# Gated linear attention with an MLP behind it: weights loaded in six parts, the quarter turn as a 128-row matmul, another order table

## The chip, the cores and the metric

The kernel runs on one core of one Trainium2 chip. The metric is the device time of one execution in microseconds, as the median of several runs; the profile is of one more execution of the same program. The engines of the core are PE (TensorE, matmuls; PEld is its loading of weights), DVE (VectorE), ACT (ScalarE), POOL (GpSimd) and SP (SyncE, which here only issues DMAs). Each engine works through its own instructions in order, and waits where an instruction needs what another engine or a DMA has yet to deliver.

## The reference

Inputs are q, k, v, a_re and a_im, each 4 x 8 x 768 x 48 (batch, heads, steps, head dimension) in fp32, a scale vector of 384 and two weight matrices of 384 x 1536 and 1536 x 384.

```python
def _attn_ref(q, k, v, a_re, a_im):
    mag = np.sqrt(a_re * a_re + a_im * a_im)
    scale = np.minimum(mag, 0.999) / (mag + 1e-06)
    a_re_n, a_im_n = (a_re * scale, a_im * scale)
    for t in range(S):
        new_re = ar * S_re - ai * S_im          # ar, ai: step t of a_re_n, a_im_n
        new_im = ar * S_im + ai * S_re
        S_re, S_im = (new_re + k_t v_t^T, new_im)
        y[:, :, t] = q_t @ S_re
...
def _moe_ref(x, g_ln, w_ch1, w_ch2):
    xn = (x - mu) / np.sqrt(var + 1e-06) * g_ln
    return x + np.maximum(xn @ w_ch1, 0.0) @ w_ch2
```

So a complex decay, one number for each head dimension and step, multiplies a state of 48 x 48 for each head; the real part of the state is read by q. The 8 heads side by side make rows of 384, which go through a layer norm, a two-layer MLP with ReLU, and a residual sum.

## The kernel before

**Tiling.** The 768 steps of a batch are cut into 6 chunks of 128 steps. Two chunks make a pair, so there are 3 pairs in a batch and 12 pairs (P = 0 to 11) in all, 24 chunks (n = 0 to 23). Each pair goes through the same stages; pair 0 is split in two halves of 4 heads for the elementwise ones (`PARTS`), so its names have .0 and .1.

**Stages of a pair**, by the names in the code:
- Loads by SP: `are`, `aim` (384 KB each for a pair), `q`, `k`, `vf` (192 KB for each chunk).
- Decay, magnitude: `ln` and `iv` on ACT (log of a_re, and its inverse by Exp), `r` (a_im / a_re), `r2`, `u` (Ln of 1 + r2, ACT), `l` and `lc` (log of the magnitude, capped, DVE), `dec` (PE, sums over the steps with triangular ones `u_e`), `en` and `e` (ACT, Exp with either sign).
- Decay, angle: `th` (Arctan, ACT), `ph` (PE, sums with `u_th`, in turns, on top of what `pick` takes from `car`, the carry of the pair before), `car` (the carry for the next pair), `sin` (ACT, Sin of the fraction of a turn read as int16), and for `cos` in pairs 0 to 3 (`QUARTER`) `qt`: a matmul that adds a quarter turn to `ph` in place, after which ACT takes Sin again. Pairs 4 to 11 use `abs` and a bias instead.
- `ke`, `qe` (k and q times the decay), `ks`, `qs` (times cos and sin, stacked as 48 + 48 rows of 128), each on DVE or POOL.
- Each chunk: `kT`, `qT` (transposes on PE) and `ksT`, `qsT` (their copies out of PSUM by DVE or ACT), or instead `ksT`, `qsT` as one transposing DMA issued by SP; `am` (8 matmuls), `atm` (times the causal mask, DVE), `gm` and `G` (state), `y` (attention output in PSUM), `x` (copy of it), `bn` (statistics), `xtr` and `xT` (transposed x).
- MLP of a pair: `mm1` in three groups of two blocks (6 matmuls of 128 x 256 each), `relu` for each group on ACT or DVE, `mm2` for each chunk in three blocks of 4 matmuls of 128 x 384, `oa` and `ot` (scale by `rstd` and add x), `st` (store).
- `dps`, `decc` take the whole decay of a pair to the state.

**Weights.** `w1b` and `w2b` hold both matrices in bf16; `wl.0` and `wl.1` load them (and cast) by one DMA each, issued by POOL. `wp` (PE) multiplies w1 by the scale vector's mean matrix `gc`, `wc` (DVE, nine instructions at L388) scales w1 and subtracts the result; mm1 of group j needs the three `wc.j`.

**Order.** Nothing is scheduled at run time. A table (`PLAN`) lists every operation by name with its engine (P, A, V, G, S for PE, ACT, DVE, POOL, SP) and, after the letter, its PSUM bank; `Graph.run` emits them in that order, so the table is the order of each engine's queue. `@name` makes an operation wait for another on top of its data (some POOL operations take turns with DVE so). `tab.log` and `tab.trig` are loads of ACT's function table: Ln and Exp need the one, Arctan and Sin the other. `warm` are fillers: a matmul of 128 x 256 on constants whose result nobody reads; they need `u_e` alone. Buffers are rings (`RINGS`, 2 to 10 of a kind).

The start of the table before, in short: pair 1's `are` first, its ln and iv, pair 0's ln and iv, a trig load with Arctan and Sin of half of pair 0, a log load, a trig load, and so on: four log and four trig loads up to pair 2's second Sin. `wl.0` is issued after `v.0`, `wl.1` after `ks.1.0.0`; all of `wp` and `wc` follow pair 0's `y`.

Of the kernel before, what the change touches and what calls it, by code (L numbers as in the profile page):

```python
# [54 lines left out]
warm.67:P4 warm.68:P4 warm.69:P4 qt.0.0:P3 dps.0:P2 cos.0.0:A3 cos.0.1:A0 ks.0.0.1:V ks.0.0.0:V ks.0.1.0:V
qs.0.1.0:V ph.1.0:P4 dec.1.0:P6 qs.0.0.0:V warm.70:P1 warm.71:P1 qT.1:P3 tab.log.2:A en.1.0:A6 u.2.0:A
ln.3.0:A iv.3.0:A e.1.0:A6 v.0:G@qs.0.0.0 decc.0:V2 ks.0.1.1:V vf.1.1:S vf.1.0:S q.2.0:S car.1.0:V4
warm.72:P1 warm.73:P1 kT.0:P2 qT.0:P1 kT.1:P0 qsT.1:V3 tab.trig.2:A sin.1.0:A4 ksT.0:V2 wl.0:G ksT.1:V0
am.1:P2 gm.0:P0 ke.1.0.1:G@ks.0.1.1 ke.1.0.0:G th.2.0:A qsT.0:V1 am.0:P6 dps.1:P1 decc.1:A1 qt.1.0:P4
l.2.0:V r.3.0:V lc.2.0:V G.0:V0 gm.1:P0 cos.1.0:A4 dec.2.0:P4 k.2.1:S tab.log.3:A e.2.0:A4 en.2.0:A4  # L60
atm.0:V6 atm.1:V2 G.1:V0 r2.3.0:V k.2.0:S are.4.0:S ph.2.0:P6 y.1:P1 aim.4.0:S ks.1.0.1:G@lc.2.0 x.1:V1
are.5.0:S ks.1.0.0:G y.0:P2 kT.3:P3 x.0:V2 ksT.3:V3 u.3.0:A tab.trig.3:A sin.2.0:A6 wp.2:P0 wc.2.1:V0
wc.2.0:V0 xtr.0:P1 wl.1:G xtr.1:P4 wp.0:P5 wp.1:P2 wc.2.2:V0 xT.1:V4 qt.2.0:P6 xT.0:A1 kT.2:P3 th.3.0:A
cos.2.0:A6 wc.0.2:V5 wc.0.1:V5 wc.1.2:V2 wc.0.0:V5 wc.1.1:V2 ksT.2:A3 mm1.0.2.1:P0 mm1.0.2.0:P0
qe.1.0.0:G@r2.3.0 qe.1.0.1:G qs.1.0.0:G relu.0.2:A0 ph.3.0:P6 qs.1.0.1:G qe.2.0.1:G qT.2:P3 qT.3:P4
car.3.0:A6 mm1.0.0.1:P0 mm1.0.0.0:P0 wc.1.0:V2 qsT.3:V4 sin.3.0:A6 qt.3.0:P6 qsT.2:A3 mm1.0.1.0:P4 l.3.0:V
lc.3.0:V qe.2.0.0:V aim.5.0:S v.1:G pad.qs.2:G am.3:P2 mm1.0.1.1:P4 cos.3.0:A6 bn.0:V bn.1:V relu.0.0:A0
qs.2.0.0:G@qe.2.0.0 k.3.0:S q.3.1:S relu.0.1:A4 gm.2:P6 rstd.0:G am.2:P0 mm2.0.0:P7 dec.3.0:P4 G.2:A6
atm.3:V2 y.3:P2 tab.log.4:A e.3.0:A4 x.3:A2 vf.2.0:S vf.2.1:S k.3.1:S gm.3:P6 atm.2:V0 qs.2.0.1:V y.2:P3
mm2.0.1:P7 qT.4:P2 xtr.3:P0 mm2.1.0:P1 mm2.0.2:P7 en.3.0:A4 mm2.1.1:P1 qT.5:P4 ln.4.0:A iv.4.0:A xT.3:A0  # L70
ln.5.0:A x.2:V3 dps.3:P3 ke.2.0.0:V ke.2.0.1:G ks.2.0.1:V ks.2.0.0:G@ks.2.0.1 kT.4:P5 xtr.2:P0 are.6.0:S
r.4.0:G q.3.0:S vf.3.0:S mm2.1.2:P1 bn.2:V bn.3:V iv.5.0:A rstd.1:A r.5.0:G r2.4.0:A decc.3:A3 ot.0:V7
G.3:V6 qsT.4:V2 xT.2:V0 mm1.1.2.1:P6 ksT.4:V5 qsT.5:V4 kT.5:P0 ot.1:V1 mm1.1.2.0:P6 qe.3.0.1:G ke.3.0.0:G
v.2:G mm1.1.0.1:P4 mm1.1.0.0:P4 ksT.5:V0 am.4:P2 am.5:P0 ke.3.0.1:G u.4.0:A relu.1.2:V6 mm1.1.1.1:P6
mm1.1.1.0:P6 relu.1.0:V4 mm2.2.0:P4 r2.5.0:A u.5.0:A tab.trig.4:A th.4.0:A relu.1.1:A6 th.5.0:A atm.5:V0
ph.4.0:P0 atm.4:V2 k.4.0:S y.4:P5 mm2.2.1:P4 ks.3.0.0:G ks.3.0.1:V l.4.0:V lc.4.0:V mm2.3.0:P6 mm2.3.1:P6
gm.4:P7 mm2.3.2:P6 abs.4.0:A0 sin.4.0:A0 qe.3.0.0:V qs.3.0.0:V qs.3.0.1:V dec.4.0:P2 vf.3.1:S st.0:S G.4:V7
x.4:V5 tab.log.5:A ln.6.0:A oa.3:A6 q.4.0:S v.3:G@qs.3.0.1 car.4.0:A0 mm2.2.2:P4 qT.6:P5 xtr.4:P7 y.5:P6
k.4.1:S q.4.1:S e.4.0:A2 l.5.0:V en.4.0:A2 qsT.6:V5 ot.3:G@l.5.0 ph.5.0:P0 aim.6.0:S x.5:V6 lc.5.0:V
xtr.5:P5 gm.6:P6 dps.4:P2 ot.2:V4 kT.6:P3 xT.5:V5 xT.4:A7 iv.6.0:A qe.4.0.0:G are.7.0:S ke.4.0.0:G@lc.5.0  # L80
ke.4.0.1:G r.6.0:G tab.trig.5:A cos.4.0:A ks.4.0.0:G qe.4.0.1:G decc.4:V2 mm1.2.0.1:P4 ks.4.0.1:G abs.5.0:A0
mm1.2.0.0:P4 qsT.7:S sin.5.0:A0 r2.6.0:A th.6.0:A ksT.6:V3 qs.4.0.0:G G.6:V6 mm1.2.1.0:P2 mm1.2.1.1:P2
gm.7:P6 ksT.7:S bn.5:V st.2:S relu.2.0:V4 G.7:V6 relu.2.1:V2 cos.5.0:A tab.log.6:A ln.7.0:A mm1.2.2.1:P0
mm1.2.2.0:P0 mm2.4.0:P7 mm2.5.0:P6 am.6:P4 bn.4:V rstd.2:A am.7:P2 mm2.4.1:P7 relu.2.2:V0 mm2.4.2:P7
dec.5.0:P0 atm.7:V2 iv.7.0:A u.6.0:A atm.6:V4 kT.8:P2 y.7:P3 k.5.0:S y.6:P4 e.5.0:A0 vf.4.0:S vf.4.1:S
are.8.0:S v.4:G q.5.0:S q.6.0:S st.1:S aim.7.0:S k.5.1:S x.6:A4 qe.5.0.0:G@l.6.0 mm2.5.1:P6 mm2.5.2:P6
ksT.9:S x.7:A3 q.5.1:S vf.5.0:S st.3:S aim.8.0:S en.5.0:A0 ksT.8:A2 qs.4.0.1:V l.6.0:V lc.6.0:V xtr.7:P5
qT.8:P4 xtr.6:P3 xT.6:V3 gm.8:P0 qT.9:P1 xT.7:A5 G.8:A0 oa.5:A6 dec.6.0:P2 r.7.0:G@lc.6.0 qsT.8:V4 am.8:P4
ln.8.0:A e.6.0:A2 ot.4:V7 en.6.0:A2 bn.7:V atm.8:V4 gm.9:P0 mm1.3.2.0:P6 G.9:V0 qsT.9:V1 mm1.3.2.1:P6
mm1.3.1.1:P4 y.8:P2 mm1.3.1.0:P4 k.6.1:S am.9:P0 dps.6:P3 bn.6:V iv.8.0:A relu.3.2:A6 ke.5.0.0:G vf.5.1:S  # L90
k.6.0:S q.6.1:S x.8:V2 st.4:S are.9.0:S xtr.8:P2 mm1.3.0.1:P6 mm1.3.0.0:P6 atm.9:V0 r2.7.0:A ke.5.0.1:G
u.7.0:A relu.3.1:A4 ks.5.0.1:V decc.6:V3 qe.5.0.1:V r.8.0:V relu.3.0:A6 ph.6.0:P0 vf.6.0:S y.9:P3 mm2.6.0:P4
mm2.7.0:P5 mm2.7.1:P5 x.9:A3 xtr.9:P3 mm2.6.1:P4 mm2.6.2:P4 l.7.0:V lc.7.0:V ks.5.0.0:V qs.5.0.0:V
tab.trig.6:A sin.6.0:A0 qs.5.0.1:V rstd.3:G xT.8:A2 ot.5:G th.7.0:A qT.10:P2 xT.9:V3 ke.6.0.0:V car.6.0:V0
abs.6.0:V0 mm2.7.2:P5 ph.7.0:P6 mm1.4.2.0:P0 qe.6.0.1:G@ke.6.0.0 qsT.10:A2 mm1.4.0.0:P2 mm1.4.0.1:P2
mm1.4.2.1:P0 sin.7.0:A6 bn.8:V r2.8.0:A cos.6.0:A qe.6.0.0:G qs.6.0.1:G v.5:G abs.7.0:V6 car.7.0:V6
relu.4.0:A2 mm1.4.1.0:P6 mm1.4.1.1:P6 th.8.0:A ot.6:V4 relu.4.2:V0 ot.7:V5 dec.7.0:P2 ksT.10:S gm.10:P4
am.10:P0 tab.log.7:A e.7.0:A2 relu.4.1:V6 mm2.8.0:P5 mm2.8.1:P5 ke.6.0.1:G qs.6.0.0:G ks.6.0.1:G ksT.11:S
qsT.11:S st.5:S mm2.8.2:P5 am.11:P6 bn.9:V ks.6.0.0:V G.10:A4 ln.9.0:A vf.6.1:S k.7.1:S aim.9.0:S en.7.0:A2
v.6:G@ks.6.0.0 mm2.9.0:P4 rstd.4:G atm.10:V0 dps.7:P2 y.10:P3 gm.12:P0 iv.9.0:A atm.11:V6 r.9.0:V mm2.9.1:P4  # L100
u.8.0:A x.10:A3 l.8.0:V G.12:A0 xtr.10:P1 y.11:P3 mm2.9.2:P4 q.8.0:S gm.13:P0 decc.7:A2 st.6:S q.7.0:S
bn.10:V r2.9.0:G@l.8.0 xT.10:A1 x.11:A3 lc.8.0:V G.13:V0 k.7.0:S q.7.1:S xtr.11:P6 oa.9:A4 vf.7.0:S xT.11:A6
ph.8.0:P2 qT.12:P4 qsT.12:V4 abs.8.0:V2 mm1.5.2.0:P6 mm1.5.0.1:P0 mm1.5.0.0:P0 tab.trig.7:A cos.7.0:A
sin.8.0:A2 qT.13:P4 mm1.5.2.1:P6 mm1.5.1.0:P2 relu.5.0:A0 mm2.10.0:P0 mm1.5.1.1:P2 bn.11:V ksT.13:S
# [702 lines left out]
```

## Time and profile before

| | |
|---|---|
| median of 3 runs | 193.94 us (193.87 to 194.18) |
| span of the profiled execution | 191.7 us, 5125 instructions |
| granted TensorE clock over the span | 0.986 |
| PE busy | 175.3 us (91%), 2039 matmuls |
| ACT busy | 165.2 us (86%), 234 instructions |
| DVE busy | 154.8 us (81%), 267 instructions |
| POOL busy | 109.2 us (57%), 124 instructions |
| table loads on ACT (L775) | 23, 29.5 us |
| fillers on PE (L770) | 74, 10.5 us |
| DMA by SP's queue | 34.88 MB, 87.7% of 16 engines' span |
| DMA by POOL's queue (weights) | 2.36 MB, 7.3% |

How to read it: spans are from the first to the last instruction of that execution. Busy times are unions, so an engine's instructions may overlap and add up to more. A matmul's duration contains its latency; in a row of matmuls the distance from start to start is shorter. Time an engine stands idle costs only where something late follows from it. In the groups, a line with "out<-in (shape) xN | busy, mean" gives the mean duration in ns of one instruction, and what ended the idle time ahead of them. In the windows, each engine has its busy time within a stretch and, after it, the number of its instructions; PEclk is the granted clock as a share of the full one.

### The profile page before, as it was taken

The page shows a single profiled execution, that of the slowest core. Times are in us where ns is not written, and L with a number is a line of the kernel's source. Part 1 is how long each engine was busy: PE and PEld are TensorE (multiplying, and loading weights), DVE is VectorE, ACT ScalarE, POOL GpSimd, SP SyncE. Part 2 cuts the span into 40 slices and gives each one's busy share as a digit, 9 for nine tenths or more (in the row PEclk, how much of TensorE's full clock was granted, in tenths as well). Part 3 has the DMA queues.
Part 4 walks back from the last instruction along what each step waited for, and adds up shares of the span by engine and source line. Part 5 has one row for each costly group of instructions (what it writes and reads, how often), then busy time and mean ns, then how long its engine had stood idle before and what let it go on. Part 6 is the DMA issues. An engine that isn't in the chain of part 4 may idle for free.

```text
span 191.7 us, 5125 instructions
## 1 busy us (share of the span) xinstructions
PE 175.3 (91%) x2039; PEld 132.7 (69%) x2039; DVE 154.8 (81%) x267; ACT 165.2 (86%) x234; POOL 109.2 (57%) x124
## 2 busy tenths in 40 slices
...
GB/s 151 291 244 219 236 190 203 168 218 298 184 212 237 166 163 255 192 258 211 161 169 265 167 255 152 184 288 253 204 228 153 208 145 144 248 103 165 3 129 118
DMA packets 132104, 37.56 MB, mean 196 GB/s; under 512 B 127088, under 2 KB 131696, under 8 KB 132080
## 3 DMA queue, kind: packets, MB, share of 16 engines
q1 hardware_dynamic: 130128, 34.88, 87.7%
q0 software_dynamic: 1952, 2.36, 7.3%
q8 instruction: 16, 0.26, 0.5%
...
## 4 chain that ended last, share of the span: by engine, by line
PE 38%; ACT 27%; DVE 16%; issue 8%; DMA 4%; POOL 3%; SPq 1%; DVEq 0%; POOLq 0%; ACTq 0%
PE banks L741 14%; PE banks L720 9%; ACT h L731 5%; ACT L775 4%; DVE w1b L388 3%; DMA qsT<-qs 3%; PE banks L477 2%; PE banks L616 2%; DVE l L466 2%; ACT r L462 2%; ACT en L481 2%; PE banks L496 2%; PE banks L593 2%; ACT r L458 2%; DMA are<-in_a_re_dram 2%
## 5 line engine op out<-in xcount | busy, mean ns | idle before, releaser
L741 PE MATMUL banks<-w2b,h 128*128 128x384 bf16 x288 | 54.9, 326 | 0.3 <-ACT h L731 0.2
L720 PE MATMUL banks<-xT,w1b 128*128 128x256 bf16 x432 | 51.9, 272 | 0.8 <-ACT trig L514 0.5
L720 PEld LDWEIGHTS <-w1b 128*128 128x128 bf16 x432 | 41.2, 98 | 7.7 <-DVE xT L291 1.3
L741 PEld LDWEIGHTS <-h 128*128 128x128 bf16 x288 | 26.0, 97 | 14.3 <-ACT h L731 0.8
L294 DVE TENSOR_TENSOR atm<-banks,mask 128x1024 bf16<-128x1024 f32 x24 | 28.7, 1217 | 5.2 <-PE banks L616 2.8
L731 ACT ACTIVATE h<-banks 128x1024 bf16<-128x1024 f32 x24 | 24.1, 1023 | 8.7 <-PE banks L720 8.5
L775 ACT ACT_TABLE_LOAD x23 | 29.5, 1283 | 1.2 <-PEq L791 0.8
L294 POOL TENSOR_TENSOR ks<-ke,trig 128x768 bf16<-128x768 bf16 x14 | 22.8, 1640 | 8.8 <-DVE ke L294 2.8
L294 POOL TENSOR_TENSOR qs<-qe,trig 128x768 bf16<-128x768 bf16 x11 | 18.0, 1641 | 12.3 <-DVE ot L755 5.0
L294 POOL TENSOR_TENSOR ke<-k,en 128x384 bf16<-128x384 f32 x18 | 16.5, 930 | 11.8 <-DMA vf<-in_v_dram 10.3
L294 POOL TENSOR_TENSOR qe<-q,e 128x384 bf16<-128x384 f32 x16 | 14.6, 921 | 12.2 <-ACT e L481 5.9
L733 DVE TENSOR_SCALAR h<-banks 128x1024 bf16<-128x1024 f32 x12 | 14.5, 1215 | 4.9 <-PE banks L720 4.9
L753 POOL TENSOR_TENSOR ot<-ot,x 128x384 f32<-128x384 f32 x8 | 7.3, 916 | 14.6 <-ACT ot L746 13.6
L616 PE MATMUL banks<-qsT,ksT 128*128 128x128 bf16 x192 | 14.3, 219 | 1.4 <-DVE ksT L291 1.2
L616 PEld LDWEIGHTS <-ksT 128*128 128x128 bf16 x192 | 12.1, 98 | 3.4 <-DVE ksT L291 1.4
L496 PE MATMUL banks<-th,u_th 128*128 128x384 f16 (+1 forms) x52 | 12.4, 325 | 2.2 <-ACT th L485 2.2
L679 DVE BATCH_NORM_STATS2 stats<-x 128x6 f32<-128x384 bf16 x24 | 13.1, 547 | 0.0
L755 DVE SCALAR_TENSOR_TENSOR ot<-banks,rstd,x 128x384 f32<-128x384 f32 x16 | 9.6, 609 | 4.1 <-DMA out_dram<-ot 2.9
L466 DVE SCALAR_TENSOR_TENSOR l<-r,w 128x768 f16<-128x768 f16 (+1 forms) x13 | 11.5, 892 | 1.6 <-ACT r L462 1.6
L770 PE MATMUL banks<-u_e 128*128 128x256 f16 x74 | 10.5, 302 | 2.2 <-POOL u_e L328 2.2
L477 PE MATMUL banks<-l,u_e 128*128 128x384 f16 (+1 forms) x52 | 10.4, 327 | 2.2 <-DVE l L469 1.3
L448 ACT ACTIVATE w<-are 128x768 f32<-128x768 f32 (+1 forms) x13 | 10.3, 796 | 2.2 <-DMA are<-in_a_re_dram 2.2
...
## 6 DMA issues: line engine op xcount, KB each, us to landing
...
```

The lines of the kernel that those rows point to most:

```text
L294: {"DVE": nc.vector, "POOL": nc.gpsimd}[eng(name)].tensor_tensor(**kw)
L466: nc.vector.scalar_tensor_tensor(out=S_("l"), in0=S_("r2"), scalar=0.5, in1=S_("w"), op0=ALU.mult, op1=ALU.add)
L477: nc.tensor.matmul(heads(ps[:, c]), lhsT=u_e[:, c, j], rhs=step(T("l", P), j), start=(j == 0), stop=(j == R - 1))
L496: nc.tensor.matmul(heads(ps[:, c]), lhsT=u_th[:, c, j], rhs=step(T("th", P), j), start=False, stop=(j == R - 1), skip_group_check=True)
L616: nc.tensor.matmul(ps[:, h], lhsT=T("ksT", n)[:, h], rhs=T("qsT", n)[:, h], start=True, stop=True)
L679: nc.vector.bn_stats(out=T("stats", n), in_=T("x", n))
L720: nc.tensor.matmul(ps[:, jj], lhsT=w1b[:, dc, ts(gi * JG + jj, C)], rhs=T("xT", P)[:, dc].rearrange("p c t -> p (c t)"), start=(dc == 0), ...
L731: act(out=dst, in_=src, func=AF.Relu)
L733: nc.vector.tensor_scalar(out=dst, in0=src, scalar1=0.0, scalar2=None, op0=ALU.max)
L741: nc.tensor.matmul(bank(f"o.{n}")[:, 0:DM], lhsT=T("h", P)[:, j, ts(c, C)], rhs=w2b[:, j], start=(j == 0), stop=(j == NJ - 1))
L770: g.add(f"warm.{i}", lambda i=i: nc.tensor.matmul(bank(f"warm.{i}")[:, 0:256], lhsT=u_e[:, 0, 0], rhs=u_e[:, 1].rearrange("p j t -> p (j t ...
L775: g.add(f"tab.{nm}.{i}", lambda tab=tab: nc.scalar.preload_act_table_set(tab))
```

## The change

Five things are changed, the last of them in the table alone:

1. `wl` becomes six DMAs: `wl.0` to `wl.2` load a third of w1's columns each, `wl.3` to `wl.5` a third of w2's rows. `wp.j` needs only `wl.j`, and block `part` of mm2 only `wl.(3 + part)`.
2. `qt` uses all 128 rows of `pick` and `qrow` instead of row 64 alone; `qrow` is therefore set to zero first.
3. 72 fillers are defined, and the table holds all 72; it held 74.
4. Table loads have one running number in the order table; there are 19 of them.
5. The order table is another one: order, engines and banks. Transposes by DMA are 22 (25 before), stacks transposed on PE 26 (23); `ksT` on DVE 11 (6), on ACT 1 (4); `decc` all 8 on DVE (5 of 8 on ACT before); `relu` 26 on ACT, 10 on DVE (24, 12); `car` 6 on ACT, 3 on DVE (3, 6); `v` 4 on DVE, 1 on ACT, 7 on POOL (1, 3, 8); smaller shifts in others.

The old names wl.0 and wl.1 stood for whole matrices; the new ones are parts.

```diff
-    g.add("qrow", lambda: nc.gpsimd.memset(qrow[ds(HALF, 1)], 0.25), needs=["ue"])
+    g.add("qrow", lambda: [nc.gpsimd.memset(qrow, 0.0), nc.gpsimd.memset(qrow[ds(HALF, 1)], 0.25)],
+          needs=["ue"])
...
-    g.add("wl.0", lambda: nc.gpsimd.dma_start(
-        out=w1b, in_=moe_w_ch1.rearrange("(dc p) j -> p dc j", p=C)))
-    g.add("wl.1", lambda: nc.gpsimd.dma_start(
-        out=w2b, in_=moe_w_ch2.rearrange("(jc p) e -> p jc e", p=C)))
+    for i in range(NG):
+        g.add(f"wl.{i}", lambda i=i: nc.gpsimd.dma_start(
+            out=w1b[:, :, ts(i, 512)], in_=moe_w_ch1.rearrange("(dc p) j -> p dc j", p=C)[:, :, ts(i, 512)]))
+        g.add(f"wl.{NG + i}", lambda i=i: nc.gpsimd.dma_start(
+            out=w2b[:, ts(i, JG)], in_=moe_w_ch2.rearrange("(jc p) e -> p jc e", p=C)[:, ts(i, JG)]))
...
-        g.add(o, wp, needs=["wgc", "wl.0"], ps=(o, 1))
+        g.add(o, wp, needs=["wgc", f"wl.{jb}"], ps=(o, 1))
...
-                        nc.tensor.matmul(ps[:, c], lhsT=pick[ds(HALF, 1)], rhs=qrow[ds(HALF, 1), 0:W],
+                        nc.tensor.matmul(ps[:, c], lhsT=pick, rhs=qrow[:, 0:W],
...
-                    needs=[f"relu.{P}.{part}", "wl.1"] + ([f"mm2.{n}.{part - 1}"] if part else []),
+                    needs=[f"relu.{P}.{part}", f"wl.{NG + part}"] + ([f"mm2.{n}.{part - 1}"] if part else []),
...
-    for i in range(240):
+    for i in range(72):
         g.add(f"warm.{i}", lambda i=i: nc.tensor.matmul(
```

The new order table from its start to pair 0's first mm1, without the fillers and the memsets, engine by engine:

```
ACT   tab.log.0 ln.0.1 ln.0.0 iv.0.1 iv.0.0 ln.1 iv.1 r2.0.0 r2.0.1 u.0.1 u.0.0 u.1 ln.2 en.0.1 iv.2 en.0.0
      e.0.1 e.1 e.0.0 en.1 u.2 | tab.trig.1 th.0.0 th.0.1 th.1 sin.0.0 sin.0.1 th.2 cos.0.0 cos.0.1 |
      tab.log.2 ln.3 en.2 iv.3 e.2 qsT.0 car.1 | tab.trig.3 sin.1 sin.2 cos.1 x.0 cos.2 x.1 th.3 xT.0 xT.1
DVE   uth r.0.0 r.0.1 r.1 r2.1 l.0.1 l.0.0 lc.0.1 lc.0.0 l.1 lc.1 wgc r.2 ke.0.0 r2.2 decc.1 decc.0 l.2 qe.1.0
      qe.0.0 lc.2 car.0.0 car.0.1 qe.0.1 ks.0.1.1 qs.0.1.1 ks.0.0.1 ks.0.0.0 qs.0.0.1 qs.0.0.0 wc.1.0 wc.1.2
      wc.1.1 wc.0.1 wc.0.0 wc.0.2 ksT.0 qsT.1 ksT.1 atm.0 atm.1 G.0 ks.1.1 ks.1.0 qs.1.1 qs.1.0 G.1 ksT.2 ksT.3
PE    42 fillers dec.0.1 dec.0.0 dec.1 dps.1 dps.0 ph.0.0 ph.0.1 qt.0.0 qt.0.1 ph.1 wp.1 dec.2 wp.0 qT.0 kT.0
      qT.1 kT.1 am.0 ph.2 am.1 gm.0 qt.1 y.0 qt.2 wp.2 y.1 xtr.0 gm.1 kT.3 kT.2 xtr.1 qT.2 qT.3 mm1.0.0.1
POOL  ue qrow ... wl.1@r2.2 wl.0 pick ke.0.1@lc.2 wl.2@qs.0.0.0 qs.0.1.0 ks.0.1.0 v.0 r.3 qe.1.1 ke.1.0 ke.1.1
      v.1@qs.1.0 wl.3 r2.3 wl.4 qe.2.1 wl.5
```

Between dec.0.0 and dec.1 stand 3 fillers, between dec.1 and dps.1 six, between dps.0 and ph.0.0 seventeen, and four more single or in twos up to kT.0. At the end of the table, the last stack to be transposed by DMA is qs.11: `qs.11.0.0` on DVE, `qsT.22` and `qsT.23` by SP right behind it, with five blocks of mm1 and one of mm2 between it and `am.22` on PE.

More of the change, by code (lines that the diff above doesn't have):

```diff
@@ L55 @@
[L55 to L104, printed above, removed]
```

159 lines of the change are left out of this document (103 added, 56 removed).

## The prediction

> **What bounds the kernel now.** First the busy time of each engine by stretches of 10 us, then the chain of waits for the pace of the matmuls, then the timeline of the first 50 us.
>
> ```profile
> core 0: us, PE busy (x) PEld busy (x) DVE busy (x) ACT busy (x) POOL busy (x), PEclk, DMA share, GB/s
> 0.00:10.00 10.00, 5.35 (x33) 3.91 (x34) 3.26 (x8) 6.92 (x10) 7.01 (x30) 1.00 0.88 222
> 10.00:20.00 10.00, 7.42 (x82) 5.98 (x80) 8.22 (x16) 9.91 (x17) 1.15 (x1) 1.00 1.08 231
> 20.00:30.00 10.00, 6.67 (x97) 4.89 (x95) 9.86 (x21) 9.86 (x15) 5.34 (x6) 0.97 1.07 210
> 30.00:40.00 10.00, 9.95 (x90) 5.98 (x89) 8.37 (x15) 9.35 (x11) 9.68 (x9) 0.86 1.15 186
> ...
> 80.00:90.00 10.00, 9.79 (x150) 8.19 (x147) 9.06 (x18) 9.97 (x15) 5.59 (x7) 1.00 0.96 215
> ...
> 150.00:160.00 10.00, 9.92 (x126) 7.23 (x125) 5.89 (x10) 8.94 (x13) 7.80 (x8) 1.00 0.90 178
> ```
>
> From 30 us on PE looks full. A modelled busy time is not PE at its pace, so I take the pace from long runs in the chain:
>
> ```profile
> 95.38 3.93 PE banks L720 x36
> ...
> 108.13 0.45 PE banks L593 x8
> ...
> 183.79 3.92 PE banks L741 x24
> 187.73 0.62 DVE ot L755
> ```
>
> 36 matmuls of mm1 in 3.93 us are 0.109 each, 24 of mm2 in 3.92 are 0.163, 8 transposes in 0.45 are 0.056 (am has the same pace). With these, and 0.65 for a dec, 0.97 for a ph, 0.40 for a y, 0.26 for a gm, 0.33 for a qt, 0.65 for a wp, all of PE's work without the fillers of L770 is 158.3 us. Pair 0's first mm1 starts at 37.4 (timeline below), when 13.4 us of it are done; 144.9 remain. 37.4 + 144.9 = 182.3, but the last mm2 ends at 187.7, so 5.4 us are lost on the way, and 4.0 follow (ot, its store): 37.4 + 144.9 + 5.4 + 4.0 = 191.7, the span. There are three things that can change: the start of mm1, PE's work, and the loss.
>
> ```profile
> 7.91 1.28 ACT L775 ACT_TABLE_LOAD   x1
> 9.21 0.52 ACT L485 ACTIVATE th<-r 128x384 f16<-128x384 f16 x1
> ...
> 24.05 8.44 SPq L404 DMA_DIRECT2D k<-in_k_dram  x2
> ...
> 35.07 2.06 DVE L388 SCALAR_TENSOR_TENSOR w1b<-w1b,gln,banks 128x512 bf16<-128x512 bf16 x3
> 37.45 1.48 PE L720 MATMUL banks<-xT,w1b 128*128 128x256 bf16 x12
> ```
>
> ACT sets both start and loss. It is busy 9.91, 9.86 and 9.35 of 10 us before mm1 and 9.97 still at 80 to 90. Added up in the order table, the ACT instructions ahead of pair 0's first mm1 last 37.8 us, ahead of pair 2's 70.1, ahead of pair 5's 110.6, beside PE work of 13.4, 42.8 and 81.4. Durations overlap: ACT's add up to 179 in all but cover 165.2, so I multiply by 0.92. Between pair 0's and pair 3's first mm1, ACT then needs 44.6 us (48.5 of durations) for 43.1 of PE; the trace shows 45.0 (37.4 to 82.4). From 150 us on ACT has air, and PE alone counts.
>
> **The change, part by part.**
>
> *Order table: ACT.* 19 table loads for 23: 4 x 1.283 = 5.1 us off, all ahead of pair 2's second Sin, since Ln and Exp of pairs 0, 1 and 2 now run under one load and both parts of pair 0's phase under the next. Engine swaps, by the group rows: three ksT copies (1.016) leave, also five decc (0.32), two v (0.83), two rstd (0.50), one oa (0.58) and one G (0.49): 8.4 off; one qsT (1.01), two relu (1.02), three car (0.48), one r2 (0.85) and one x (0.48) come: 5.8 on. Sum 5.1 + 8.4 - 5.8 = 7.7 us less of durations.
>
> *Order table: DVE.* On: five ksT (0.68), five decc (0.33), three v (0.55), two qe, two ks, one each of qs, ot, G: 10.6. Off: two relu (1.22), three car (0.56), one each of ke, r, r2, x: 7.0. DVE gets 3.6 us more.
>
> *Order table: PE.* Three more stacks are turned by PE and not by DMA: 24 x 0.056 = 1.35 us. PE's work is 159.65.
>
> *Start of mm1.* In the new order, durations ahead of pair 0's first mm1 are 33.8 on ACT (37.8 before), 30.5 on DVE (33.6), PE work 14.3 (13.4). The queues, walked through: the first are lands as before (192 KB instead of 384), ACT starts at 4.4, and its 33.8 less the first load are 32.5 x 0.92 = 29.9; before, 36.5 x 0.92 + 4.2 = 37.8 stands against 38.6, the end of the last in that list (ksT.2), so 0.8 were waits. 4.4 + 29.9 = 34.3, plus 1 us of waits: 35.3. DVE can end its products of pair 0 at about 22.5, as the ACT durations up to cos.0.1 are 20.3 with the first load's 1.28: 4.4 + 19.0 x 0.92 = 21.9, and a product or two. Then it has six w1b corrections (L388, 4.03 for x6), three copies of 0.65, two atm of 1.2, G and four products of pair 1: 22.5 + 4.0 + 2.0 + 2.4 + 0.5 + 2.3 = 33.7, then PE turns two stacks (0.9): 34.6, and about ten handovers of 0.1 between engines: 35.6. I take 36.4, 0.8 later than either, for what such a walk leaves out. Bounds: 35.3, and 37.4 as now.
>
> *Loss.* Ahead of pair 2's and pair 5's first mm1 ACT now has 66.4 and 107.6, beside PE work of 44.3 and 83.5; from pair 0's to pair 5's it needs 67.9 us for 69.2 of PE. Before, it was 67.0 for 68.0, but from 4 us higher and with stretches in which it fell behind (pair 1 to pair 3: 30.3 for 28.3). DVE's 73.8 x 0.92 = 67.9 is equal to that. PE thus stays the slowest. Of the 5.4 lost I give back 1.5 (44.6 - 43.1, what ACT's queue forces up to pair 3) and keep 3.9. Bounds: 2.8 (all that is lost before pair 4 gone) and 5.4. The end adds 0.4: qsT.22 is issued behind DVE's last qs and has PE work of 3.9 - 0.6 = 3.3 us to hide behind, where a turn by DMA takes 3.4 (page, qsT 3.4) and once 4.85; bounds 0 and 1.6.
>
> *Weights in six parts.* Four more issues on POOL at 1.04 (1.00 and 1.08 in the timeline) are 4.2 us, in front of ke, qs and ks of pairs 0 to 2. POOL is busy 1.15 and 5.34 of 10 in the two stretches where it matters; its queue to pair 1's ke ends at 22.5 + 1.0 + 1.8 + 0.8 + 0.5 + 1.8 + 0.9 + 1.9 = 31.2 (a part, two half products, v, a pad, r, qe, two ke), and DVE, by the walk above, asks for it at 31.4. That cover is 0.2 us; each us beyond it is paid. Two w1 parts now land before 22 us and six of nine corrections are done before pair 0 is turned, where now they lie at 35.1 to 41.3 between xT and mm1. A part is a third of 9.9 us by its bytes, 3.3, and at most the whole 9.9; I take 5, as loads of SP run beside. What SP's queue loses, 8.44 us for two k issues while the whole w1b flies, should be about a third.
>
> *Quarter turn by 128 rows.* 10 matmuls of the same columns; one row or 128 stream alike (L521 at 0.162, L496 with 128 rows at 0.1625). One memset of 0.42 on POOL before 5 us. Nothing; POOL waits there for DVE's u_th until 3.4 us and needs `one` only at 9.3.
>
> *Fillers.* 72 for 74. On PE they have no wait but the first, so 42 run in one piece to about 8.5 us (29 now last 4.88 from 2.22, 13 more at 0.109), whatever stands between them in the table. Nothing, unless the clock falls (rival 2).
>
> **Sum.** 36.4 + (159.65 - 14.3) + 3.9 + 0.4 + 4.0 = 190.05. The runs' median is 193.94 beside the profiled span of 191.7, so 2.2 lie outside it; with these the time is 192.3 us, 0.8% less.
>
> **Rivals.**
>
> 1. *A late part of w1 stops DVE and PE: slower.* wp.1 stands on PE before dec of pair 2, and the six corrections on DVE before ksT.0. If a part takes the whole's 9.9 us, the parts issued at 15.6 (behind r2 of pair 2, by the walk) and 16.6 land at 25.5 and 26.5, the corrections end at 30.2 instead of 26.5, and all moves by 3.7: 192.3 + 3.7 = 196.0. It decides the sign from a landing 1.5 us later than the slot, some 7 us after issue. For: a DMA share of 1.08 and 1.07 there. Against: two parts are two thirds of its bytes, and w1b held up SP's queue (8.44 us for two k issues), not the other way round.
>
> 2. *Half clock before mm1.* The rows give 0.97 and 0.86 at 20:40: half clock for 0.6 + 2.8 = 3.4 us from 29.3, after a stretch of transposes and waits. In the new order PE is nearly idle from 8.5 to 11.3 (fillers out, lc of pair 0 comes at 11.3 by the walk) and mostly transposing from 24 to 27. The first costs 0.65 (dec of pair 1 doubled, the Exp behind it on ACT), the second up to 1.5 (kT, am, ph before atm.1): 192.3 + 2.15 = 194.4, or 193.0 with the first alone. Against: the old order paid such a fall too.
> The Trainium skill ("TensorE: Matmul & The Clock Gate", What's actually happening) halves the clock after an idle window of about 3.4 us, and its Part 4 does not count PE transposes as busy. The trace agrees on the 3.4 us of half clock.
>
> 3. *DVE takes ACT's place: slower.* DVE has 3.6 us more, and between pair 4's and pair 5's mm1 16.8 x 0.92 = 15.5 for 14.7 of PE. Then start and loss stay: 37.4 + 145.35 + 5.4 + 0.4 + 4.0 = 192.55, time 194.7. It decides if DVE's idle time before 40 us, 10.3 now, stays above 9.5. Against: 3.1 us less on DVE ahead of mm1.
>
> 4. *Table loads weigh more than their row.* If each load also emptied the engine behind it, ACT would gain twice 5.1, and DVE alone would set the start, 35.3, with a loss of 2.8: 187.85, time 190.1. Against: the load at 7.91 ends at 9.19 and Arctan starts at 9.21.
> The Trainium skill ("ScalarE: Activation LUTs", What ACT_TABLE_LOAD costs) adds a drain of about 1.38 us to 1.283, 2.66 in all; the trace has the 1.283 and no drain.
>
> 5. *The change doesn't do what it says:* the fillers are not wider spaced on PE at all; contained in 2.
>
> **How the numbers follow.** Forecast 0.42, rival 1 0.16, rival 2 0.15, rival 3 0.20, rival 4 0.06, anything else 0.01 (slower). What this kernel's measurement can tell from no change is 0.2%, 0.39 us. The forecast's own range is 191.0 to 193.6 (start 35.3 to 37.4, loss 2.8 to 5.4, not all at once); it is faster but for 0.02. Rival 2 is faster in a third (0.05), same in 0.05, slower in 0.05. Rival 3 comes out the same in 0.03, else it and rival 1 are slower. Faster 0.40 + 0.05 + 0.06 = 0.51; same 0.02 + 0.05 + 0.03 = 0.10; slower 0.05 + 0.16 + 0.17 + 0.01 = 0.39. The range, 190.3 to 196.2, reaches from rival 4 to rival 1.
>
> **What would show it.** Right: first L720 at 35.3 to 37, 19 rows of L775, ACT idle more than 6 us from 40 to 150 in all (4.5 now), first L388 before 25 us. The loss is wrong if the last L741 ends over 150.5 us after the first L720. Rival 1: L384 waiting for DMA w1b. Rival 2: PEclk under 0.9 before 30 us. Rival 3: DVE 9.8 of 10 from 20 to 110 while ACT and PE wait for it.

## The result, and the profile after

The changed kernel takes 192.51 us (median of 20 runs, 191.47 to 194.02), the kernel before, on the same chip, 193.91 us (20 runs, 193.37 to 194.82). The ratio is 0.9931, with a 95% interval of 0.9915 to 0.9946: 1.3 us faster (1.0 to 1.6 us). Executions over 1.5% longer than the shortest of their kernel are left out of the ratios here and below; in one of them, beside the last experiment, the kernel before took 299.22 us at a granted clock of 0.564. The profiled execution took 192.54 us with a span of 190.8 us. Its line numbers are those of the kernel before less 1 for the matmuls and weights (mm1 is L719, mm2 L740, w1's corrections L387, wp L383, table loads L774).

First the busy time of each engine by stretches of 10 us, as it was read before.

```profile
core 0: us, PE busy (x) PEld busy (x) DVE busy (x) ACT busy (x) POOL busy (x), PEclk, DMA share, GB/s
0.00:10.00 10.00, 6.15 (x42) 4.93 (x43) 2.26 (x4) 5.75 (x10) 6.24 (x27) 1.00 0.86 215
10.00:20.00 10.00, 7.30 (x76) 5.35 (x76) 8.45 (x22) 9.39 (x16) 3.10 (x5) 0.83 1.06 216
20.00:30.00 10.00, 7.06 (x70) 4.85 (x68) 8.23 (x18) 9.85 (x14) 6.92 (x8) 1.00 1.20 215
30.00:40.00 10.00, 9.71 (x145) 8.11 (x143) 10.00 (x16) 9.07 (x14) 6.61 (x8) 1.00 0.90 182
```

The granted clock now falls between 10 and 20 us (0.83) and not between 20 and 40. DVE, not ACT, is the full engine of 30 to 40. From 40 to 150 us ACT is busy for 102.33 of 110 us, so it stands idle for 7.7 us; before it was 4.5.

The timeline, at the places that the prediction's sum is made of:

```profile
20.08 6.17 SPq L403 DMA_DIRECT2D k<-in_k_dram  x2
...
24.09 2.06 DVE L387 SCALAR_TENSOR_TENSOR w1b<-w1b,gln,banks 128x512 bf16<-128x512 bf16 x3 [0.42 <-PE banks L383]
...
27.03 2.06 DVE L387 SCALAR_TENSOR_TENSOR w1b<-w1b,gln,banks 128x512 bf16<-128x512 bf16 x3 [0.88 <-PE banks L383]
...
36.64 1.47 PE L719 MATMUL banks<-xT,w1b 128*128 128x256 bf16 x12
...
183.08 3.41 PE L740 MATMUL banks<-w2b,h 128*128 128x384 bf16 x20
```

Pair 0's first mm1 starts at 36.64, the last mm2 ends at 183.08 + 3.41 = 186.49. With the forecast's 145.35 us of work in between, 186.49 - 36.64 - 145.35 = 4.5 us are lost on the way, and 4.3 follow:

| us | before | forecast | after |
|---|---|---|---|
| start of mm1 | 37.4 | 36.4 | 36.6 |
| PE's work from there (by pace) | 144.9 | 145.35 | 145.35 |
| lost on the way, the wait for qsT.22 included | 5.4 | 4.3 | 4.5 |
| after the last mm2 | 4.0 | 4.0 | 4.3 |
| span | 191.7 | 190.05 | 190.8 |
| around the span | 2.2 | 2.2 | 1.7 |

The waits of PE, in us in total, times, longest. Two of them are for weights, one for `pick`, which POOL now makes behind two parts of w1, and one for the last stack that is turned by DMA:

```profile
PE banks L383 <- DMA w1b<-in_moe_w_ch_dram: 1.5, 2, 1.3
PE banks L491 <- POOL pick L335: 0.9, 1, 0.9
...
PE banks L740 <- DMA w2b<-in_moe_w_ch_dram: 0.3, 1, 0.3
...
PE banks L615 <- DMA qsT<-qs: 0.3, 1, 0.3
```

The chain that ended last, by engine, from the pages of the kernel before and of the changed one:

```profile
PE 38%; ACT 27%; DVE 16%; issue 8%; DMA 4%; POOL 3%; SPq 1%; DVEq 0%; POOLq 0%; ACTq 0%
```

```profile
PE 50%; DMA 15%; DVE 9%; ACT 6%; POOL 6%; SPq 6%; issue 4%; POOLq 0%; DVEq 0%; ACTq 0%
```

ACT's share of the chain fell from 27% to 6%, DMA's rose from 4% to 15%. Up to 46 us the new chain does not run over the first mm1. From 11 us on it runs over SP's issues, the load of `aim` for pair 3, POOL and the landing of a part of w2, for which PE waits 0.3 us (start, length, what):

```profile
16.58 9.14 DMA aim<-in_a_im_dram
25.72 0.87 POOL ks L291
...
37.20 1.42 POOL r L291
38.61 7.71 DMA w2b<-in_moe_w_ch_dram
46.37 1.46 PE banks L740 x8
```

The experiments ask three things of it: what ACT's time was worth, whether DVE took its place, and what the small edits (parts, quarter turn, fillers) do alone and in this order.

### The profile page after: what moved, and what is told of

It is laid out like the page before. It is cut to its first block, busy times and chain, and to the rows that moved or that the text cites. A ratio compares the mean times of both kernels' runs of the same rounds, so it can differ in the third digit from the quotient of the medians.

```text
span 190.8 us, 5173 instructions
## 1 busy us (share of the span) xinstructions
PE 174.8 (92%) x2061; PEld 134.5 (70%) x2061; DVE 154.8 (81%) x283; ACT 157.3 (82%) x217; POOL 109.9 (58%) x128
## 4 chain that ended last, share of the span: by engine, by line
PE 50%; DMA 15%; DVE 9%; ACT 6%; POOL 6%; SPq 6%; issue 4%; POOLq 0%; DVEq 0%; ACTq 0%
PE banks L740 17%; PE banks L719 14%; DMA aim<-in_a_im_dram 5%; DMA w2b<-in_moe_w_ch_dram 4%; PE banks L592 4%; SPq L403 3%; PE banks L615 3%; PE banks L495 3%; DMA are<-in_a_re_dram 2%; PE banks L476 2%; DMA qsT<-qs 2%; DVE atm L291 2%; DMA q<-in_q_dram 2%; POOL r L291 2%; PE banks L665 2%
## 5 line engine op out<-in xcount | busy, mean ns | idle before, releaser
L740 PE MATMUL banks<-w2b,h 128*128 128x384 bf16 x288 | 55.3, 326 | 0.3 <-DMA w2b<-in_moe_w_ch_dram 0.3
L719 PE MATMUL banks<-xT,w1b 128*128 128x256 bf16 x432 | 51.3, 273 | 0.9 <-ACT trig L513 0.9
L719 PEld LDWEIGHTS <-w1b 128*128 128x128 bf16 x432 | 41.4, 98 | 7.3 <-issue 0.8
L740 PEld LDWEIGHTS <-h 128*128 128x128 bf16 x288 | 25.8, 97 | 13.5 <-issue 0.4
L730 ACT ACTIVATE h<-banks 128x1024 bf16<-128x1024 f32 x26 | 26.0, 1019 | 5.7 <-PE banks L719 4.4
L291 POOL TENSOR_TENSOR ke<-k,en 128x384 bf16<-128x384 f32 x19 | 17.2, 916 | 16.8 <-DVE qs L291 5.8
L291 POOL TENSOR_TENSOR ks<-ke,trig 128x768 bf16<-128x768 bf16 (+1 forms) x12 | 18.9, 1583 | 6.6 <-DVE qs L291 2.0
L752 POOL TENSOR_TENSOR ot<-ot,x 128x384 f32<-128x384 f32 x7 | 6.4, 916 | 18.2 <-ACT ot L745 15.9
L291 POOL TENSOR_TENSOR qs<-qe,trig 128x768 bf16<-128x768 bf16 (+1 forms) x10 | 15.7, 1569 | 0.3
L754 DVE SCALAR_TENSOR_TENSOR ot<-banks,rstd,x 128x384 f32<-128x384 f32 x17 | 10.3, 610 | 6.8 <-ACT h L730 3.5
L291 POOL TENSOR_TENSOR qe<-q,e 128x384 bf16<-128x384 f32 x14 | 12.7, 918 | 4.2 <-ACT trig L513 3.4
L291 POOL TENSOR_TENSOR r<-aim,are 128x768 f16<-128x768 f32 x6 | 10.9, 1816 | 5.5 <-ACT are L449 5.4
L732 DVE TENSOR_SCALAR h<-banks 128x1024 bf16<-128x1024 f32 x10 | 12.1, 1216 | 2.0 <-PE banks L719 2.0
L769 PE MATMUL banks<-u_e 128*128 128x256 f16 x72 | 11.1, 312 | 2.2 <-POOL u_e L325 2.2
L665 PE MATMUL banks<-v,atm 128*128 128x48 bf16 x192 | 12.1, 183 | 0.1
```

Of the source, the lines that this page charges most:

```text
L291: {"DVE": nc.vector, "POOL": nc.gpsimd}[eng(name)].tensor_tensor(**kw)
L665: nc.tensor.matmul(ps[:, h], lhsT=T("atm", n)[:, h], rhs=T("v", P)[:, c, h], start=True, stop=nfirst)
L719: nc.tensor.matmul(ps[:, jj], lhsT=w1b[:, dc, ts(gi * JG + jj, C)], rhs=T("xT", P)[:, dc].rearrange("p c t -> p (c t)"), start=(dc == 0), ...
L730: act(out=dst, in_=src, func=AF.Relu)
L732: nc.vector.tensor_scalar(out=dst, in0=src, scalar1=0.0, scalar2=None, op0=ALU.max)
L740: nc.tensor.matmul(bank(f"o.{n}")[:, 0:DM], lhsT=T("h", P)[:, j, ts(c, C)], rhs=w2b[:, j], start=(j == 0), stop=(j == NJ - 1))
```

## The experiments

Each ratio is against runs of the kernel before in the same job; the changed kernel stands at 0.9931 on that scale. Where two variants are compared with each other, the difference of their ratios is taken, times 193.9 us, and its interval from both.

**The quarter turn by one row.**

```diff
-                        nc.tensor.matmul(ps[:, c], lhsT=pick, rhs=qrow[:, 0:W],
+                        nc.tensor.matmul(ps[:, c], lhsT=pick[ds(HALF, 1)], rhs=qrow[ds(HALF, 1), 0:W],
```

> The changed kernel with the quarter turn as before, by one row of pick and qrow instead of 128. Times are against the kernel before on the same chip, where the changed kernel stood at -1.4 us. My theory (the quarter turn costs the same with one row or with 128, since a 128x384 piece takes 0.32 to 0.33 us in both traces): -1.4 us, within 0.3. Rival (the 128-row form is worth something by itself, for instance by keeping the granted clock up): -1.0 us or less gain, and a fall of the clock that the changed kernel does not have.

Ratio 0.9916 (0.9890 to 0.9942), 192.43 us: the changed kernel, within the interval. The quarter turn by 128 rows costs nothing that can be seen. The clock of the profiled execution fell twice (0.83 from 10 to 20 and from 20 to 30). Its first mm1 starts at 37.48, and with 193.90 us it is the longest of the seven; the two with a mean granted clock of 0.995 and 1.000 are the shortest (191.74 and 191.89). So a second fall goes with a longer time here; which of them causes the other is not shown.

**The weights in two transfers, in the new order.**

```diff
+    g.add("wl.1", lambda: nc.gpsimd.dma_start(
+        out=w1b, in_=moe_w_ch1.rearrange("(dc p) j -> p dc j", p=C)))
+    g.add("wl.3", lambda: nc.gpsimd.dma_start(
+        out=w2b, in_=moe_w_ch2.rearrange("(jc p) e -> p jc e", p=C)))
...
-        g.add(o, wp, needs=["wgc", f"wl.{jb}"], ps=(o, 1))
+        g.add(o, wp, needs=["wgc", "wl.1"], ps=(o, 1))
```

> The changed kernel with the weights in two transfers as before, the whole of w1 issued at the place of the first part (about 16.2 us) and the whole of w2 at the place of its first part. By the rows of the kernel before, the whole of w1 lands 9.9 us after its issue, here about 26.1 us, where the first part landed at 23.2 and the second at 26.1. Theory A (the DVE queue stops at the first correction, and this is on the path): the first correction goes from 24.09 to about 26.9, less the 0.88 us wait ahead of the second three that falls away, about +1.9 us, so +0.5 us against before. Theory B (the queues take it up further on, or the SP queue is blocked for less): within 0.3 us of the changed kernel, -1.4 us.

Ratio 1.0494 (1.0460 to 1.0528), 203.73 us: 11 us slower than the changed kernel, far beyond both theories. PE's waits, and the transfers issued from 10 to 45 us (KB each, us from issue to landing):

```profile
PE banks L739 <- DMA w2b<-in_moe_w_ch_dram: 5.4, 1, 5.4
PE banks L382 <- DMA w1b<-in_moe_w_ch_dram: 2.4, 1, 2.4
```

```profile
w1b<-in_moe_w_ch_dram POOLq DMA_DIRECT2D x1, 1152.0 KB, 10.8
...
w2b<-in_moe_w_ch_dram POOLq DMA_DIRECT2D x1, 1152.0 KB, 12.8
```

I had reckoned with w1 alone. The larger part is w2: issued as one piece, it lands 12.8 us later, and PE stands 5.4 us at its first mm2, where in the changed kernel the first third was enough. A program written for two transfers would have issued them elsewhere, so 11 us is not the price of two transfers, but of taking the parts out of an order that counts on them.

**The two small edits in the old order.** Six transfers, three back to back at each of the two old places, and the quarter turn by 128 rows; the old table otherwise.

```diff
-ksT.0:V2 wl.0:G ksT.1:V0
+ksT.0:V2 wl.2:G wl.0:G wl.1:G ksT.1:V0
...
-xtr.0:P1 wl.1:G xtr.1:P4
+xtr.0:P1 wl.3:G wl.4:G wl.5:G xtr.1:P4
```

> The kernel before, in its own order, with only the two small edits: the weights in six transfers, three back to back at each of the two places, and the quarter turn by 128 rows. Theory (the gain is the order table's): 0 us, within 0.3. Rival (the parts are worth something in any order): w1's first part lands 3 to 5 us earlier than the 32.55 us of the whole, the first correction moves by as much, and up to -1.4 us. The other way: four more POOL issues of 0.8 to 1.0 us hold up POOL, up to +1 us.

Ratio 0.9981 (0.9960 to 1.0003), 193.62 us against 193.86: no difference that the interval separates from none. Alone the parts bring next to nothing; without them the new order loses 11 us. They are what makes the order possible, not what makes it faster.

**30 more fillers.**

```diff
-    for i in range(72):
+    for i in range(102):
```

> The changed kernel with 30 more fillers (30 x 0.109 = 3.3 us at the full clock) behind the first 42 and ahead of the first decay product, so that TensorE does not stand idle from 8.4 to 11.8 us. Theory (that idle time brings the half clock of 11.96 to 15.37 us, and the doubled decay products hold ACT up by 0.58 us at 15.02 and some more): granted clock full from 5.1 us on, first mm1 at about 36.0 instead of 36.64, -1.9 to -2.2 us against before. Rival (ACT and DVE make up for it before mm1): clock full, first mm1 at 36.6, -1.4 us. If the clock falls all the same, the fall does not come from that idle time.

```profile
10.00:20.00 10.00, 7.43 (x91) 5.72 (x89) 8.75 (x22) 9.84 (x17) 3.04 (x6) 1.00 0.99 197
20.00:30.00 10.00, 7.21 (x67) 5.04 (x68) 7.77 (x17) 9.29 (x14) 6.39 (x7) 1.00 1.21 214
```

In these stretches (columns as above) the clock is full, as it should be if the fall came from PE's idle time behind the 42 fillers. It is so in more than the profiled execution: all twelve have a mean granted clock of 0.994 or more, eighteen of the changed kernel's twenty have 0.991 or less. (The profiled executions of two kernels below kept the full clock from 10 to 20 us without more fillers.) But the ratio is 0.9923 (0.9894 to 0.9952), the changed kernel's, the median 192.79 us, and first mm1 starts at 36.98 in the profiled execution. So taking the half clock of 12 to 15 us away in this manner brings nothing that can be seen. PE now waits 1.8 us for `pick` instead of 0.9; whether that takes back what the full clock gives is not separated.

**Four table loads more, from 40 to 130 us.**

```diff
-tab.log.6:A
+tab.trig.20:A tab.log.6:A
```

and the same ahead of the loads 8, 10 and 12.

> The changed kernel with four table loads put back, as many as the change takes away, each ahead of an existing one between about 55 and 125 us (a set loaded that the next load replaces: nothing computed changes). They cost ACT 4 x 1.283 = 5.1 us. Times against the kernel before, where the changed kernel stands at -1.4 us. Theory (ACT is one of two or three engines that hold TensorE up in turn, and the 7.7 us less of it brought about 1 us less lost on the way): +0.5 to +1.2 us over the changed kernel, -0.9 to -0.2 against before. Rival 1 (ACT binds throughout): +5 us, +3.7 against before. Rival 2 (DVE binds, and ACT's 7.7 us of idle time between 40 and 150 us take it up): less than +0.3 us, -1.4 to -1.1.

Ratio 1.0082 (1.0050 to 1.0114), 195.09 us: 2.9 us (2.2 to 3.6) over the changed kernel for 5.13 us of ACT, 0.57 per us (0.43 to 0.70). My theory of 0.5 to 1.2 us fell, and so did both rivals: ACT does not bind throughout, but its idle 7.7 us are not free time.

**Two table loads more before mm1.**

```diff
-tab.trig.1:A
+tab.log.20:A tab.trig.1:A
...
-tab.log.2:A
+tab.trig.21:A tab.log.2:A
```

> The changed kernel with two more table loads ahead of the first mm1: one ahead of the load at 17.75 us and one ahead of the load at 23.14 us, 2 x 1.283 = 2.57 us of ACT, which is busy for 19.2 of the 20 us from 10 to 30 us. Theory (ACT sets the start of mm1): first mm1 at about 39.2 instead of 36.64, and the time +2.3 to +2.7 us, +1.0 against before. Rival (DVE and the weights set it, ACT only comes close): first mm1 at 37.2 or earlier, time within +0.8 us, -0.6 or less against before. If a load costs more than its 1.283 us in the record, the start moves by more than 2.7 us.

Ratio 1.0026 (1.0000 to 1.0052), 194.61 us: 1.8 us (1.3 to 2.4) over the changed kernel for 2.57 us of ACT. First mm1 goes to 38.72 in the profiled execution, by 2.1 us. That is close to the theory, but not all of it is ACT's own time: PE waits 1.6 us for ACT's `e` at 29.46, and from 30.2 to 33.7 us, ahead of mm1, the clock is half a second time (0.83 from 30 to 40). Ten of the twelve executions have a mean granted clock of 0.980 to 0.982; the two at 0.990 and 0.991 are the shortest (193.47 and 193.11 us). How the loss divides between ACT and the clock is not shown. The time moves by less than the loads' own length.

**Four idle fills on DVE at the same four places.** Nothing computed changes.

```diff
+        g.add(f"dum.{i}", lambda: nc.vector.memset(scr, 0.0))
...
-tab.log.6:A
+dum.0:V tab.log.6:A
```

> The changed kernel with four idle fills of a 128x1024 f32 scratch tile on DVE, at the same four places as the four table loads of the run before it; by the rows of other 128x1024 pieces 0.7 to 1.2 us each, 2.7 to 4.9 us together (its own rows will tell). Theory (ACT and DVE both hold TensorE up in turn): about as much per us added as the four table loads. Rival 1 (DVE took ACT's place as the bound): nearly all of what is added, +2.5 us or more over the changed kernel, and three times what ACT's loads cost per us. Rival 2 (neither binds in this stretch): less than +0.3 us.

The tile's own row (ns, least, median and most; first and last start):

```profile
L774 DVE MEMSET scr<- x4: 912/912/912, 48.6 to 116.2; 128x1024 f32 x4
```

4 x 0.912 = 3.65 us on DVE. Ratio 1.0036 (1.0006 to 1.0066), 194.25 us: 2.0 us (1.4 to 2.7) over the changed kernel, 0.56 per us (0.38 to 0.74). That is the theory: within these intervals a microsecond of DVE costs as much as one of ACT.

**w1 earlier (e8_w1_early).** `pick` ahead of the first two parts, these behind the clamp of pair 1.

```diff
-wl.1:G@r2.2.0
+pick:G wl.1:G@lc.1.0
...
-pick:G
```

> The changed kernel with POOL's list changed at one place: pick is made ahead of the first two parts of w1, and these are issued behind the clamp of pair 1 (about 13.2 us) instead of behind the square of pair 2 (16.2 us). Theory (the first phase product waited 0.9 us for pick, TensorE and DVE 1.5 and 1.3 us for parts of w1, and these waits are on the path to mm1): all of them gone, first mm1 at 35.3 to 36.0 instead of 36.64, -2.0 to -2.8 us against before. Rival (ACT's own work, 9.4 of 10 and 9.85 of 10 us, sets the start): waits gone, first mm1 and time as before the edit, -1.4 us. The other way: parts issued at 13.2 us put the SP queue's k, q and aim back by up to 2 us, and -0.9 us or less gain.

Ratio 1.0112 (1.0068 to 1.0156), 195.62 us: 3.5 us slower than the changed kernel, more than even the third guess said. Its six executions lie from 193.49 to 197.79 us, and the profiled one is the shortest, so the profile shows the least of it. In it the waits for `pick` and w1 are gone and first mm1 starts at 36.03, but PE waits 1.8 us for w2, and 6.1 us are lost behind the start of mm1 (4.5 in the changed kernel). The others were not profiled.

**w2 earlier, then `pick` first, then w1 earlier too.** The three parts of w2 go ahead of pair 1's v, into POOL's idle stretch; the second kernel also has `pick` ahead of w1's parts; the third also has w1 behind the clamp of pair 1.

```diff
-v.1:G@qs.1.0.0
+wl.3:G wl.4:G wl.5:G v.1:G@qs.1.0.0
...
-wl.3:G
...
-wl.4:G
...
-wl.5:G
```

> The changed kernel with the three parts of w2 issued back to back in the stretch in which POOL stands idle (32.2 to 35.6 us, ahead of pair 1's v) instead of at 36.4, 38.6 and 40.3 us. Times against the kernel before, where the changed kernel stands at -1.4 us. Theory (TensorE's second product comes close to the landing of w2: 0.3 us of waiting in the changed kernel's profile, 0.8 with more fillers, 1.8 with w1 early, and more in the executions that are slow, whose times spread over 2.5 to 4 us where the kernel before spreads over 1.5): no wait for w2, -1.8 to -2.4 us, and a narrower spread. Rival (the parts then hold the SP queue's loads of k and q up by as much as TensorE gains): no wait for w2, and -1.4 us within 0.3.

> The run before it, with pick made ahead of the first parts of w1 in POOL's list (where these are issued stays as it is). Theory (the first phase product's 0.9 us of waiting for pick is on the path to mm1): first mm1 0.5 to 0.9 us earlier than in the run before it, and as much in the time. Rival (ACT's queue, with 9.4 of 10 and 9.85 of 10 us busy, or the parts of w1 set the start): the wait for pick gone, first mm1 and time unchanged within 0.3 us.

> The run before it, with the first two parts of w1 issued behind the clamp of pair 1 as in the run called e8_w1_early. That run lost 2.1 us between 40 and 50 us where the changed kernel lost 0.5, and 1.8 us of it is TensorE waiting for w2. Theory (its loss was w2's late landing): with w2 early, the loss is gone, and first mm1 at about 36.0 or earlier shows in the time, -2.0 to -3.0 us against before. Rival (earlier parts of w1 set the SP queue's loads back, and that costs whatever w2 does): slower than the run before it by 1 us or more.

| | ratio | median us | first mm1 | lost behind it |
|---|---|---|---|---|
| changed kernel | 0.9931 (0.9915 to 0.9946) | 192.51 | 36.64 | 4.5 |
| w2 earlier | 0.9940 (0.9913 to 0.9968) | 192.88 | 36.52 | 5.0 |
| and pick first | 0.9921 (0.9896 to 0.9947) | 192.74 | 36.02 | 5.5 |
| and w1 earlier | 1.0072 (1.0035 to 1.0110) | 195.77 | 36.33 | 11.1 |

Without a gain from an earlier w2, and with w1 earlier slower by 2.9 us, the rivals of the first and the third held. The second is not decided: first mm1 starts 0.5 us earlier, at the lower end of the theory's 0.5 to 0.9, and the 0.4 us in time lie within the interval. Transfers issued from 30 to 40 us, in the changed kernel, with w2 earlier, and with all three edits:

```profile
w2b<-in_moe_w_ch_dram POOLq DMA_DIRECT2D x2, 384.0 KB, 7.0
...
aim<-in_a_im_dram SPq DMA_DIRECT2D x1, 384.0 KB, 6.3
```

```profile
w2b<-in_moe_w_ch_dram POOLq DMA_DIRECT2D x3, 384.0 KB, 8.3
...
aim<-in_a_im_dram SPq DMA_DIRECT2D x1, 384.0 KB, 11.9
```

```profile
w2b<-in_moe_w_ch_dram POOLq DMA_DIRECT2D x3, 384.0 KB, 10.2
...
aim<-in_a_im_dram SPq DMA_DIRECT2D x1, 384.0 KB, 13.3
```

The wait for w2 is gone, but aim of pair 4, issued beside the parts, now takes 11.9 us to land instead of 6.3. In the third kernel 13.3 us are too many, and the wait runs through four engines (waits from 40 to 60 us):

```profile
POOL r L291 <- DMA aim<-in_a_im_dram: 5.1, 1, 5.1
ACT r L457 <- POOL r L291: 3.8, 1, 3.8
...
PE banks L476 <- DVE l L468: 3.4, 1, 3.4
DVE l L465 <- ACT r L461: 3.1, 1, 3.1
```

That execution took 198.78 us, the longest of its eight (the others took 193.78 to 196.47), so it and the 11.1 us of the table show this chain at its largest; whether the others wait there too is not shown. The Trainium skill ("DMA: Bandwidth & Descriptors", Issuing engines are not separate DMA queues) says that transfers run on the same 16 engines whichever queue issued them, and interleave there. The rows agree: what POOL's parts gained, SP's load lost. Why the first parts of w1, 2.5 us earlier (at 13.7 instead of 16.2), cost so much, long after they have landed (by about 23.3 us), is not settled: SP's next load, aim of pair 3, took some 4 us to issue in both kernels (1.1 in the changed one), but SP issued aim of pair 4 only 0.4 and 1.5 us later than in the changed kernel.

**Four table loads more in the kernel before**, ahead of its own loads at 45.85, 73.9, 99.4 and 117.0 us.

```diff
-tab.log.4:A
+tab.trig.20:A tab.log.4:A
```

> The kernel before, in its own order, with four more table loads ahead of its loads at 45.85, 73.9, 99.4 and 117.0 us: the same 4 x 1.283 = 5.1 us of ACT that cost the changed kernel 2.9 us at 46.6, 73.3, 96.1 and 113.7 us. The kernel before left ACT 4.5 us of idle time between 40 and 150 us, the changed one 7.7. Theory A (ACT was nearer to being the bound before, and the new order made room on it): more than in the changed kernel, +3.5 to +5 us. Theory B (work put into a written order costs 0.5 to 0.6 of its length in either, whatever the idle time says): +2.5 to +3.2 us. Theory C (ACT did not bind the kernel before in this stretch, and its four loads less were not what made the change faster): under +2 us.

Ratio 1.0246 (1.0226 to 1.0265), 198.54 us: +4.8 us (4.4 to 5.1) for 5.13 us of ACT, 0.93 per us (0.85 to 1.0). Theory A. The chains of this kernel and of the changed one with its four loads:

```profile
ACT 49%; PE 37%; issue 6%; DVE 4%; DMA 2%; DVEq 0%; ACTq 0%
```

```profile
PE 47%; ACT 21%; DVE 15%; DMA 6%; issue 4%; SPq 3%; POOL 1%; DVEq 0%; ACTq 0%; POOLq 0%
```

In the old order four more loads make ACT half of the chain; in the new one PE stays the largest, and DVE keeps a share beside ACT.

None of the variants beats the changed kernel by more than the interval.

## Why the prediction was right, point by point

The forecast was 192.3 us; the time is 192.5. The span was forecast 0.75 us too short, and 0.5 us less than before lay around it in the profiled execution, so the closeness is partly luck: 0.2 us too late a start, 0.2 more lost, 0.3 more at the end. The signs named for it came: first mm1 at 36.64, 19 table loads, 7.7 us of idle time on ACT, the first correction at 24.09, the last mm2's end 149.85 us after the first mm1's start. Those of rivals 1 and 2 came as well, a wait for w1 and a clock of 0.83, but not their prices.

*ACT sets both start and loss: right for the kernel before, half of it for the changed one.* Before, a microsecond put into ACT's middle stretch came out as 0.93 of time; in the new order it is 0.57, and ahead of mm1 1.8 of 2.57, with a second fall of the clock in it. ACT is the engine that the change relieved: 157.3 us busy for 165.2, 19 table loads for 23.

*Loss from 5.4 to 3.9: right in direction and nearly in size* (4.5, of which 0.3 is the wait for qsT.22). That 7.7 us less of ACT bring so little looks odd beside the 0.93 that the same kernel pays for each us added. The two can fit together: behind the start of mm1, time taken from ACT can bring back no more than what PE loses there, 5.4 us, while time added has no such limit. What I mis-sized is the slope in the new order: I read ACT's idle 7.7 us as room, expected four loads to cost 0.5 to 1.2 us there, and they cost 2.9.

*The order table and its table loads.* With four loads more, from 46 to 114 us, the changed kernel is 0.8% slower than the kernel before (1.0050 to 1.0114), and still 1.6% faster than the kernel before with four more of its own (1.0246). But the loads that the change takes away stood elsewhere, ahead of mm1: eight loads start before 37.45 us in the kernel before, four before 36.5 us in the changed one. Nearer to that are the two loads put back ahead of mm1, which alone use the gain up (1.0000 to 1.0052). That the relief of ACT carries the whole gain would fit all this. It is argued, not shown: no run takes the four loads out of the old order, or puts all four back where they stood.

*DVE +3.6 us: wrong.* DVE is busy 154.8 us in both profiles. The swaps came, but two groups of the kernel before ran longer than they had to, and I took their means over. The clamps (L469, now L468) take 351 ns instead of 451, 1.3 us over 13 of them; with the 0.9 us of u_th that is 2.2 of the 3.6; the rest is not broken down. The scaling of u_th took 1.19 us:

```profile
2.11 0.42 POOL L355 MEMSET car<- 128x384 f16 x1
2.20 1.19 DVE L333 TENSOR_SCALAR u_th<-u_e 128x512 f16<-128x512 f16 x1 [2.20 <-POOL u_e L328]
```

and takes 0.29 now that POOL's next memset is ordered behind it:

```profile
2.20 0.29 DVE L330 TENSOR_SCALAR u_th<-u_e 128x512 f16<-128x512 f16 x1 [2.20 <-POOL u_e L325]
2.56 0.89 POOL L350 MEMSET qrow<- 128x384 f16 x2 [0.39 <-DVE u_th L330]
```

The Trainium skill ("SBUF — State Buffer", Who interferes with whom) says that a DVE instruction in a 2-port mode, which this operation can enter, and POOL shut each other out of a shared pair of ports for a whole instruction. The rows agree: the same operation, 0.9 us longer beside memsets.

*Rival 3, DVE takes ACT's place: half of it.* Not as the bound, but level within the intervals: 0.56 per us on DVE, 0.57 on ACT. The start and the loss did improve, which rival 3 ruled out.

*Weights in six parts, hidden with 0.2 us of cover: right in sum, not in its numbers.* The first two parts land 7.0 and 9.0 us after issue (issued at 16.2 and 17.2, landed at 23.2 and 26.1), not 5. Six corrections end at 29.1, not 26.5. PE waits 1.5 and DVE 1.3 us for them, as in rival 1, and yet mm1 starts only 0.24 us later than the 36.4 I took, which had 0.8 us of margin over the walk. Rival 1's price of one us for one us did not come. What I missed is that the order depends on the parts.

*Quarter turn and fillers, nothing: right* (0.9916 and 0.9923 beside 0.9931). Rival 2's fall came at its first place, from 11.96 to 15.37 us. I had priced it at 0.65; fillers that take it away bring nothing, but they also make PE wait longer, so its cost stays open. The fall at the second place, priced at up to 1.5, did not come in the profiled execution. Where one came from 21.9 to 25.3 us, with the quarter turn by one row, first mm1 starts 0.84 us later than in the changed kernel's profile.

*Rival 4, loads that weigh more than their row: fell.* Of each microsecond of added load 0.57 to 0.93 came out as time, never more.
